# A fused pooled-attention and two-expert kernel: one of three Strassen sums moved from GpSimd to VectorE, attention steps split in two, loads handed out later

## The chip, the core and the metric

The kernel runs on one core of a Trainium2 chip. The time is device microseconds (us) of one execution; the number to predict is the median of the changed kernel's runs. TensorE is called PE (its weight loads PEld), VectorE DVE, ScalarE ACT, GpSimd POOL, SyncE SP. SP issues nearly all DMAs. Each engine works through its own queue in the order in which the program was written.

## The reference

```
k_p, v_p = k and v averaged over groups of 8 positions      # 8 batches, 8 heads, 576 x 64 -> 72 x 64
attn = softmax(q @ k_p.T / 8) @ v_p                          # per batch and head
x = attn as 4608 tokens x 512
h = x @ w_in                      # 512 x 2048
x = (h * clip(h + 3, 0, 6) / 6) @ w_out
out = (silu(x @ w_gate) * (x @ w_val)) @ w_out2              # d_ff 1536
```

All inputs arrive as 64-bit floats in raw words; the kernel itself turns weights into 32-bit floats ("rescale", then "join").

## The kernel before

Every matrix product is done in split form: an operand is a high part, rounded to the matmul's format, and a low part (the rest), and three matmuls make one product. Every operand is therefore written twice: ACT copies the high part, DVE (or POOL) subtracts to get the low part.

The program has four stages, one after the other on PE.

1. **Startup**: attention of the first 512 tokens.
2. **The up stage**: the first layer's up product for nine blocks of 512 tokens, 16 pieces f of 128 hidden units each (`up`, L587, twelve 512-column matmuls). While block j is multiplied, the attention of block j+1 is woven in. After each piece ACT forms relu (`act1`, L598, tile `t`) and DVE the gated value (L600, tile `g`), which is stored to DRAM.
3. **The down stage**: the first layer's down product (L850), 63 steps i = 7j + n, in Strassen form with seven products per block. The sums S1 to S4 of quarters of g are needed. In the kernel before, S3 = g11 - g21 is formed by POOL in the up stage, in the tile before it is stored (L602, for the 8 pieces f < 8 of each block); S2, S1 and S4 are formed by DVE in the down stage (`sum_b`, L828).
4. **The second expert** (L671 and what is around it), which the diff doesn't touch.

The attention of a unit (a head pair p of a batch b, 64 to 256 tokens) is cut into steps with letters: S scores, X subtract the maximum, A exponential, N row sums, M scale on POOL (L522), E the split of the last 16 columns, T transposes on PE, U and L the split of the transposed weights, V the value product on PE (L565 to L568, bank `psv`), W the high part of its result on ACT (L576), Y the low part on DVE (L580, tile `x`). There is a single `psv` bank, so the value product of a unit waits for the Y of the unit before. Once per head pair there are K steps (RK sums the keys on POOL, L382; K transposes them) and value steps: R0 sums the values on POOL (tile `v_in`, L425, L432), R1 their tail (tile `vts`, L425), R splits both (ACT L144 and L441, DVE L145 and L442, tiles `vst` and `vtl`), and then the loads for the second head pair after it are issued. A table `when` gives each letter a place (units later, place within the unit), and the steps are sorted by it; `attn_slot` deals them out, two slots per piece f, by their PE steps S, V, T. The weights of later stages are prepared besides (`prep_step`): loads, rescale on ACT, join on DVE (L136, L139), sums on POOL (L202, L207), a high-part copy of 1792 elements on ACT (L261), a low part on DVE (L264), a store.

The lines around the gate in the main loop:

```
up(hp, wu[f], x_tile(j))
attn_slot(j, 2 * f)
g = act1(f, hp)
attn_slot(j, 2 * f + 1)
```

Of the kernel before, what the change touches and what calls it, by code (L numbers as in the profile page):

```python
# [8 lines left out]
F32 = mybir.dt.float32  # L9
# [14 lines left out]
def kernel(  # L24
# [28 lines left out]
    P = 128  # L53
# [20 lines left out]
    t_p = l1.enter_context(tc.tile_pool(name="t", bufs=3))  # L74
# [13 lines left out]
    def big_w(name):  # L88
        return wu_p.tile([P, BIG], F32R, tag="w4", name=name)

# [56 lines left out]
    class Weights:  # L147
# [14 lines left out]
        def convert(self):  # L162
# [63 lines left out]
    def prep_step(u, step):  # L226
# [21 lines left out]
        elif step == 2:  # L248
            q = prep_t["f", u] = q7_p.tile([P, 8, WH], F32, tag="q7", name="q7")
            for s, at in prep_t.pop(("q", u)):  # L250
                join(s, q[:, at].bitcast(I32), 2)
        elif step == 3:
# [5 lines left out]
        elif step == 4:  # L258
            q, t = prep_t["f", u], s7_p.tile([P, 7, 2, WH], F32R, tag="s7", name="s7")
            prep_t["s", u] = t  # L260
            nc.scalar.copy(out=t[:, :, 0], in_=q[:, :7])  # L261
        else:
            q, t = prep_t.pop(("f", u)), prep_t.pop(("s", u))
            nc.vector.tensor_tensor(out=t[:, :, 1], in0=q[:, :7], in1=f32(t[:, :, 0]), op=ALU.subtract)  # L264
# [107 lines left out]
    def reduce_k(b, p):  # L372
        kp = a_p.tile([SP_, 2, D], F32, tag="kp", name="kp", bufs=1)
# [63 lines left out]
    def split_v(b, p):  # L437
        w, m = vst_t[p], vm_t.pop((b, p))
        split(w[:, 0], w[:, 1], m, nc.vector)
        w, vt = vtl_t[p][:, D:], vt_t.pop((b, p))  # L440
        nc.scalar.activation(out=w, in_=vt[:, 0], func=ACTF.Copy, scale=1.0 / POOL)  # L441
# [82 lines left out]
    def split_tail(u, engine):  # L524
        e, _, et, _ = e_t[u]
        qt, ni = e.shape[0], e.shape[1]
        tail = e[:, :, P:K2]
        r = et.rearrange("q i (r s) -> q i r s", r=3)[:, :, :, :TAIL]
        nc.scalar.copy(
            out=r[:, :, 0::2].bitcast(F32R), in_=tail.unsqueeze(2).to_broadcast([qt, ni, 2, TAIL])  # L530
        )
        engine.tensor_tensor(out=r[:, :, 1], in0=tail, in1=r[:, :, 0], op=ALU.subtract)
# [288 lines left out]
    SLOT = {"11": 0, "S1": 0, "12": 1, "S4": 1, "S3": 2, "22": 3, "S2": 3}  # L821
# [8 lines left out]
    def split_b(i, c):  # L830

        j, n = divmod(i, 7)
        if j < NB:
            t = gb[i, c] = gb_p.tile([P, 2, CB, MB], F32R, tag="gb", name="gb")
# [62 lines left out]
    for j in range(NB):  # L897
# [38 lines left out]
    }  # L936
    events = []
    for i in range(NU):
# [4 lines left out]
        stages = [(what, i) for what in "SXANMETULVWY"]  # L943
# [4 lines left out]
        if i in first_in_head:  # L948
            stages += [(what, first_in_head[i]) for what in ("RK", "K", "R0", "R1", "R")]
# [17 lines left out]
    for i, u in enumerate(units):  # L967
        h, sg = head_no[u[:2]], seg_no[seg_of[u]]
        before(*((what, i) for what in "SXANMETULVWY"))
        before(("P", sg), ("S", i))  # L970
        before(("RK", h), ("K", h), ("S", i))
        before(("R0", h), ("R", h), ("V", i))
# [7 lines left out]
        if h + 1 < len(heads):  # L980
            before(("K", h), ("RK", h + 1))
# [279 lines left out]
```

## Time and profile before

| what | us |
|---|---|
| runs of the kernel before | 1894.56, 1894.41, 1892.64 (median 1894.41) |
| the profiled execution, its own time | 1893.08 |
| its span, first to last instruction | 1891.3 |
| up stage, from 50 to 721 | 671.0, of it PE busy 567.05 |
| down stage, from 721 to 1084 | 363.0, of it PE busy 362.77 |
| second expert, from 1084 to 1891 | 807.0, of it PE busy 793.21 |

An engine's busy time beside the length of a stage tells how far that engine is from filling it. The granted clock is the mean over a stretch; TensorE runs at one of two levels, 1.2 and 2.4 GHz, and 1.00 means the higher one all the time.

### The profile page before, as it was taken

What the parts mean: (1) busy time and instruction counts of PE and PEld (TensorE: products, weight loads), DVE (VectorE), ACT (ScalarE), POOL (GpSimd) and SP (SyncE); (2) the same over time, 40 slices, a digit from 0 to 9 for tenths busy, and PEclk for the clock granted to TensorE, in tenths of its full rate; (3) what the DMA queues carried; (4) which work ended last, traced back from release to release, by engine and by line L of the source; (5) the groups of instructions that cost most, each with busy time, mean ns of one, the idle gap of its engine ahead of it and who ended that gap; (6) DMA issues with size and microseconds to landing.
All of it is one profiled execution on the core that took longest, in us unless ns stands there. A gap on an engine that the chain in (4) does not pass through costs nothing.

```text
span 1891.3 us, 31360 instructions
## 1 busy us (share of the span) xinstructions
PE 1750.4 (93%) x11241; PEld 1641.4 (87%) x11241; DVE 1334.1 (71%) x2398; ACT 758.3 (40%) x1689; POOL 695.3 (37%) x899
## 2 busy tenths in 40 slices
PE   5877878878797989999999989999999999999999
PEld 4666757767676879999999989999999999999999
DVE  6665757778776726778878666866867767668666
ACT  6553434444453524554555422422423324224223
POOL 5445366576765310000000036155054153351460
PEclk7889989989898999999999989999999999999999
DMA  7744667766765788654555377787887887977876
GB/s 167 170 128 140 199 186 208 246 192 218 227 200 168 257 299 324 224 182 173 179 181 195 108 279 255 260 315 237 292 287 247 292 291 239 318 264 249 291 245 218
DMA packets 235836, 432.52 MB, mean 229 GB/s; under 512 B 86688, under 2 KB 168608, under 8 KB 218528
## 3 DMA queue, kind: packets, MB, share of 16 engines
q1 hardware_dynamic: 229184, 425.00, 68.4%
q10 hardware_dynamic: 6496, 5.51, 0.9%
q8 instruction: 89, 1.46, 0.3%
q14 instruction: 67, 0.55, 0.1%
HBM read 326.11 MB, written 104.33 MB: 228 GB/s over the span
## 4 chain that ended last, share of the span: by engine, by line
PE 71%; DMA 8%; DVE 8%; POOL 4%; ACT 3%; SPq 3%; issue 3%; POOLq 0%; DVEq 0%; ACTq 0%
PE b L671 42%; PE b L850 17%; PE h L587 10%; DMA g<-g 3%; DMA q_in<-in_q_dram 2%; DVE g L600 2%; ACT t L598 1%; POOL vts L425 1%; SPq L366 1%; DMA wstg<-in_moe_w_out_dram 1%; POOL v_in L425 1%; POOL g L602 1%; POOL q L207 1%; SPq L118 1%; DMA wstg<-in_moe_w_gate_dram 1%
## 5 line engine op out<-in xcount | busy, mean ns | idle before, releaser
L671 PE MATMUL b<-xc,wr 128*128 128x384 f32 x3024 | 529.4, 336 | 10.2 <-DMA wr<-sup 6.5
L671 PEld LDWEIGHTS b<-xc,wr 128*128 128x128 f32 x3024 | 527.2, 189 | 11.3 <-ACT xc L144 9.4
L587 PE MATMUL h<-x,wu 128*128 128x512 f32 x1728 | 458.8, 420 | 6.9 <-DVE g L600 6.9
L718 POOL TENSOR_TENSOR s<-s,c 128x384 f32<-128x384 f32 x144 | 142.4, 1012 | 770.1 <-ACT s L716 770.1
L587 PEld LDWEIGHTS h<-x,wu 128*128 128x128 f32 x1728 | 340.7, 203 | 79.4 <-DVE g L600 8.3
L680 DVE TENSOR_TENSOR c<-c,b 128x384 f32<-128x384 f32 x504 | 265.2, 552 | 178.9 <-PE b L671 153.6
L850 PEld LDWEIGHTS b<-gb,pw 128*128 128x128 f32 x3024 | 362.3, 191 | 0.6 <-DVE gb L145 0.3
L850 PE MATMUL b<-gb,pw 128*128 128x256 f32 x3024 | 362.7, 283 | 0.1
L671 PE MATMUL b<-wr,gc 128*128 128x256 f32 x2268 | 265.6, 279 | 0.0
L671 PEld LDWEIGHTS b<-wr,gc 128*128 128x128 f32 x2268 | 265.4, 188 | 0.0
L144 ACT CAST gb<-gq 128x512 fp32r<-128x512 f32 x252 | 155.4, 621 | 175.8 <-PE b L850 154.4
L145 DVE TENSOR_TENSOR gb<-gq,gb 128x512 fp32r<-128x512 f32 x252 | 168.5, 689 | 74.4 <-ACT gb L144 73.1
L600 DVE SCALAR_TENSOR_TENSOR g<-t,h 128x512 f32<-128x512 f32 x144 | 98.0, 682 | 141.9 <-ACT t L598 98.7
L725 POOL TENSOR_TENSOR gf<-s,c 128x384 f32<-128x384 f32 x144 | 168.2, 1192 | 67.2 <-DVE c L680 64.5
L144 ACT CAST gc<-gf 128x768 fp32r<-128x768 f32 x126 | 105.6, 838 | 186.9 <-POOL gf L725 100.9
L716 ACT ACTIVATE s<-c 128x384 f32<-128x384 f32 x144 | 73.5, 526 | 204.5 <-DVE c L680 203.3
L145 DVE TENSOR_TENSOR gc<-gf,gc 128x768 fp32r<-128x768 f32 x126 | 133.8, 1095 | 15.6 <-ACT gc L144 13.9
L598 ACT ACTIVATE t<-h,half 128x512 f32<-128x512 f32 x144 | 98.5, 684 | 114.3 <-PE h L587 99.5
L565 PE MATMUL psv<-aT,vst 128*128 128x256 f32 (+3 forms) x96 | 32.6, 339 | 90.3 <-DVE x L580 80.5
L565 PEld LDWEIGHTS psv<-aT,vst 128*128 128x128 f32 x96 | 19.6, 204 | 101.3 <-DVE x L580 31.6
L602 POOL TENSOR_TENSOR g<-g 128x256 f32<-128x256 f32 x72 | 57.1, 795 | 121.5 <-DVE g L600 112.3
L522 POOL TENSOR_TENSOR e<-e,sm 96x288 f32<-96x288 f32 (+3 forms) x85 | 58.8, 692 | 106.6 <-DVE sm L518 69.9
(106 smaller groups left out, 1824.5 us busy)
## 6 DMA issues: line engine op xcount, KB each, us to landing
wr<-sup SPq DMA_DIRECT2D x72, 1024.0 KB
wr<-sdn SPq DMA_DIRECT2D x84, 768.0 KB
wr<-sup SPq DMA_DIRECT2D x72, 768.0 KB
gq<-g SPq DMA_DIRECT2D x36, 1024.0 KB
g<-g SPq DMA_DIRECT2D x128, 256.0 KB
sup<-s SPq DMA_DIRECT2D x12, 1792.0 KB
wstg<-in_moe_w_out_dram SPq DMA_DIRECT2D x56, 256.0 KB
sw<-s SPq DMA_DIRECT2D x8, 1792.0 KB
```

What stands on the lines that cost most here:

```text
L144: nc.scalar.copy(out=hi, in_=src)
L145: lo_engine.tensor_tensor(out=lo, in0=src, in1=f32(hi), op=ALU.subtract)
L587: nc.tensor.matmul(out=ps, lhsT=w(kt, wh), rhs=x(kt, xh), start=first and n == 0, stop=last and n == 3 * len(kts) - 1,)
L598: nc.scalar.activation(out=t, in_=ps, func=ACTF.Relu, bias=half, scale=1.0 / 6.0)
L600: nc.vector.scalar_tensor_tensor(out=g, in0=t, scalar=1.0, in1=ps, op0=ALU.min, op1=ALU.mult)
L602: nc.gpsimd.tensor_tensor(out=g[:, MB:], in0=g[:, :MB], in1=g[:, MB:], op=ALU.subtract)
L671: nc.tensor.matmul(out=ps, lhsT=w(wh), rhs=x(xh), start=first and n == 0, stop=last and n == 2)
L680: add = lambda dst, a, b: nc.vector.tensor_tensor(out=dst, in0=a, in1=b, op=ALU.add)
L716: nc.scalar.activation(out=g[q], in_=c[q], func=ACTF.Sigmoid)
L718: nc.gpsimd.tensor_tensor(out=g[q], in0=g[q], in1=c[q], op=ALU.mult)
L725: nc.gpsimd.tensor_tensor(out=gf[p][:, GP[TURN[q]], f], in0=g[q], in1=c[q], op=ALU.mult)
L850: nc.tensor.matmul(out=ps[:, d], lhsT=w[:, CB * c + k, wh, P * d:P * (d + 1)], rhs=g[:, gh, k], start=what == place and (c, d, k, m) == (0 ...
```

## The change

It is made of these parts.

- S3 is no longer formed by POOL before the store. `store_g` now stores the plain g21, and `sum_b` forms S3 on DVE in the down stage, in two halves at n = 0 of every block.
- The gate (`gate1`) is written after the second attention slot of a piece, its relu (`act1`) before it as it was. The ring of `g32` goes from 3 to 4 tiles and that of `t` from 3 to 2. The joined first-layer weights take their place in the ring `gb` and no longer in the ring of `t`.
- Value steps: R keeps the two ACT copies, a new step Q holds the two DVE low parts. Tail steps: E keeps the ACT copy, a new step F the low part. RK, M, R0, R1, R and W get other places in `when`; the ring of `kp` goes from 1 to 2.
- Weight preparation: six steps become nine; the join goes over two slots, the high-part copy and the low part are cut into 4 and 3 of their 7 planes.
- Key, tail and value loads go into the list `later`, eight steps behind RK or Q, and are issued from there. In the last block the load of the fourth weight operand is moved behind the loop, and the load of g21 forward.

```diff
-    t_p = l1.enter_context(tc.tile_pool(name="t", bufs=3))
+    t_p = l1.enter_context(tc.tile_pool(name="t", bufs=2))
...
-                t = t_p.tile([P, WC], F32, tag="t", name="w32")
+                t = f32(new_gb().rearrange("p a k n -> p (a k n)")[:, :WC])
...
-        for step, off in enumerate((0, 3, 4, 5, 6, 7)):
+        for step, off in enumerate((0, 3, 4, 5, 6, 7, 8, 8, 9)):
...
-            nc.scalar.copy(out=t[:, :, 0], in_=q[:, :7])
+            q, t, part = prep_t["f", u], prep_t["s", u], slice(0, 4) if step == 5 else slice(4, 7)
+            nc.scalar.copy(out=t[:, part, 0], in_=q[:, part])
...
-        kp = a_p.tile([SP_, 2, D], F32, tag="kp", name="kp", bufs=1)
+        kp = a_p.tile([SP_, 2, D], F32, tag="kp", name="kp", bufs=2)
...
     def split_v(b, p):
+        nc.scalar.copy(out=vst_t[p][:, 0], in_=vm_t[b, p])
+        nc.scalar.activation(
+            out=vtl_t[p][:, D:], in_=vt_t[b, p][:, 0], func=ACTF.Copy, scale=1.0 / POOL
+        )
+
+    def split_v_lo(b, p):
         w, m = vst_t[p], vm_t.pop((b, p))
-        split(w[:, 0], w[:, 1], m, nc.vector)
+        nc.vector.tensor_tensor(out=w[:, 1], in0=m, in1=f32(w[:, 0]), op=ALU.subtract)
...
-    def act1(f, ps):
+    def act1(ps):
         t = t_p.tile([P, N], F32, tag="t", name="t")
         nc.scalar.activation(out=t, in_=ps, func=ACTF.Relu, bias=half, scale=1.0 / 6.0)
-        g = t_p.tile([P, N], F32, tag="g32", name="g32")
+        return t
+
+    def gate1(t, ps):
+        g = t_p.tile([P, N], F32, tag="g32", name="g32", bufs=4)
         nc.vector.scalar_tensor_tensor(out=g, in0=t, scalar=1.0, in1=ps, op0=ALU.min, op1=ALU.mult)
-        if f < NP1:
-            nc.gpsimd.tensor_tensor(out=g[:, MB:], in0=g[:, :MB], in1=g[:, MB:], op=ALU.subtract)
         return g
...
-            "S2": ("22", "S3", ALU.subtract), "S1": ("S2", "11", ALU.add), "S4": ("12", "S2", ALU.subtract),
+            "S3": ("11", "21", ALU.subtract), "S2": ("22", "S3", ALU.subtract), "S1": ("S2", "11", ALU.add), "S4": ("12", "S2", ALU.subtract),
...
-        "RK": (-2, 14), "K": (-1, 11), "P": (-1, 4), "S": (1, 0), "X": (1, 1), "A": (1, 15), "N": (1, 18),
-        "M": (1, 19), "E": (2, 15), "T": (3, 16), "U": (4, 2), "L": (4, 15), "V": (5, 14),
-        "W": (5, 14.5), "Y": (5, 20.5), "R0": (1, 21), "R1": (2, 15), "R": (2, 19),
+        "RK": (-2, 3), "K": (-1, 11), "P": (-1, 4), "S": (1, 0), "X": (1, 1), "A": (1, 15), "N": (1, 18),
+        "M": (2, 2), "E": (2, 15), "F": (2, 18), "T": (3, 16), "U": (4, 2), "L": (4, 15), "V": (5, 14),
+        "W": (5, 16.5), "Y": (5, 20.5), "R0": (0, 21), "R1": (1, 15), "R": (2, 3), "Q": (2, 15),
...
+            later.append((done[0] + 8, lambda h=h: load_k(*heads[h], nc.sync)))
+
+    def next_v(i):
+        for load in (load_vtail, load_v):
+            for h in next_heads(i):
+                later.append((done[0] + 8, lambda load=load, h=h: load(*heads[h], nc.sync)))
...
-            ("g", 0, 0), ("w", 0, 0), ("w", 0, 1), ("g", 0, 3), ("w", 1, 0), ("w", 1, 1), ("w", 2, 0),
-            ("w", 2, 1), ("g", 0, 1), ("w", 3, 0), ("w", 3, 1), ("g", 0, 2)]))
+            ("g", 0, 0), ("w", 0, 0), ("w", 0, 1), ("g", 0, 3), ("w", 1, 0), ("w", 1, 1), ("g", 0, 2),
+            ("g", 0, 1), ("w", 2, 0), ("w", 2, 1)]))
...
-                g = act1(f, hp)
+                t = act1(hp)
                 attn_slot(j, 2 * f + 1)
+                g = gate1(t, hp)
...
-        for n in (4, 5, 6):
+        for n in (3, 4, 5, 6):
...
-        sums_at = {1: (("S2", 0), ("S2", 1)), 2: ((), ("S1", 0)), 3: (("S1", 1), ()),
+        sums_at = {0: (("S3", 0), ("S3", 1)), 1: (("S2", 0), ("S2", 1)), 2: ((), ("S1", 0)), 3: (("S1", 1), ()),
```

The order of PE's own instructions is the same in both kernels. What moves is the order on DVE, ACT, POOL and SP. The first place is on DVE, in the attention of batch 6, ahead of the low part of a value result (`x`), for which PE's next value product waits. Before, from the subtraction of the maximum (`e`) to that low part:

```order
L494 TENSOR_TENSOR e_5592<-pss_5588,mx_5590 128x144
L458 STREAM_TRANSPOSE qT_5598<-q_in_5475 128x448
L559 TENSOR_TENSOR aT_5594<-pst_5554,aT_5594 128x192
L532 TENSOR_TENSOR et1_135<-e_5504,et1_135 128x16
L516 TENSOR_REDUCE sm_5612<-e_5592 128x2
L517 TENSOR_SCALAR sm_5612<-sm_5612 128x2
L518 RECIPROCAL sm_5612<-sm_5612 128x2
L145 TENSOR_TENSOR vst1_124<-v_in_4897,vst1_124 128x128
L442 SCALAR_TENSOR_TENSOR vtl1_128<-vts1_132,vtl1_128 32x64
L580 TENSOR_TENSOR x_5155<-psv_5600,x_5155 128x192
L600 SCALAR_TENSOR_TENSOR g32_5667<-t_5665,h_5625 128x512
```

With the change, the same head pair's value steps and the low part of the unit that follows them:

```order
L506 TENSOR_TENSOR e_5570<-pss_5566,mx_5568 128x144
L470 STREAM_TRANSPOSE qT_5579<-q_in_5455 128x448
L452 TENSOR_TENSOR vst1_124<-v_in_4873,vst1_124 128x128
L454 SCALAR_TENSOR_TENSOR vtl1_128<-vts1_132,vtl1_128 32x64
L576 TENSOR_TENSOR aT_5572<-pst_5538,aT_5572 128x192
L620 SCALAR_TENSOR_TENSOR g32_5595<-t_5564,h_5525 128x512
L139 TENSOR_SCALAR q7_5522<-wstg_5280 128x512
L142 SCALAR_TENSOR_TENSOR q7_5522<-wstg_5280,q7_5522 128x512
L549 TENSOR_TENSOR et1_135<-e_5488,et1_135 128x16
L528 TENSOR_REDUCE sm_5593<-e_5570 128x2
L529 TENSOR_SCALAR sm_5593<-sm_5593 128x2
L530 RECIPROCAL sm_5593<-sm_5593 128x2
```

The next row on DVE is the low part of `x`. The value low parts (`vst`, `vtl`) stood right ahead of it before; now eight rows stand between, among them a gate and half a join.

The second place is on POOL, for the second and the third head pair of the same batch (values `v_in`, tails `vts`; the scaling M writes `e`). Before:

```order
L425 TENSOR_TENSOR v_in_4897<-v_in_4897 128x64
L432 TENSOR_TENSOR v_in_4897<-v_in_4897,vmask_133 128x128
L602 TENSOR_TENSOR g32_5585<-g32_5585 128x256
L425 TENSOR_TENSOR vts1_132<-vts1_132 96x256
L425 TENSOR_TENSOR vts1_132<-vts1_132 96x128
L425 TENSOR_TENSOR vts1_132<-vts1_132 96x64
L202 TENSOR_TENSOR q7_5536<-q7_5536 128x256 x4
L522 TENSOR_TENSOR e_5592<-e_5592,sm_5612 128x144
L425 TENSOR_TENSOR v_in_5569<-v_in_5569 128x256
```

With the change:

```order
L439 TENSOR_TENSOR v_in_4873<-v_in_4873,vmask_133 128x128
L534 TENSOR_TENSOR e_5411<-e_5411,sm_5438 128x144
L432 TENSOR_TENSOR vts1_132<-vts1_132 96x256
L432 TENSOR_TENSOR vts1_132<-vts1_132 96x128
L432 TENSOR_TENSOR vts1_132<-vts1_132 96x64
L549 TENSOR_TENSOR et0_134<-e_5411,et0_134 128x16
L432 TENSOR_TENSOR v_in_5548<-v_in_5548 128x256
L432 TENSOR_TENSOR v_in_5548<-v_in_5548 128x128
L432 TENSOR_TENSOR v_in_5548<-v_in_5548 128x64
L439 TENSOR_TENSOR v_in_5548<-v_in_5548,vmask_133 128x128
L534 TENSOR_TENSOR e_5488<-e_5488,sm_5517 128x144
```

The subtraction on `g32` and the block of preparation sums have left this stretch, and the values of the third head pair (`v_in_5548`) stand ahead of the scaling of `e_5488`. Its unit's scaling wrote `e_5504` before, and that one and the next unit's (`e_5592`) came ahead of the third pair's values (`v_in_5569`).

## Rows read from the trace of the kernel before

**Rows 1.** Windows: length, busy PE, PEld, DVE, ACT, POOL (instructions), granted clock, DMA share, GB/s

```profile
50.00:721.00 671.00, 567.05 (x2806) 466.51 (x2807) 449.00 (x1023) 296.16 (x841) 356.43 (x550) 0.92 0.66 206
721.00:1084.00 363.00, 362.77 (x3025) 362.15 (x3024) 284.59 (x406) 185.43 (x299) 0.00 (x0) 1.00 0.53 187
```

**Rows 2.** Waits of PE, 50 to 721: total us, times, longest

```profile
PE psv L565 <- DVE x L580: 80.5, 37, 7.4
PE psk L406 <- POOL kp L382: 8.7, 6, 2.4
PE h L587 <- DVE g L600: 6.9, 3, 4.1
```

**Rows 3.** Waits of ACT and of DVE, 50 to 721

```profile
ACT vtl L441 <- POOL vts L425: 40.6, 20, 6.5
ACT s L261 <- POOL q L207: 21.8, 7, 5.2
...
DVE g L600 <- DMA g<-g: 37.3, 9, 8.6
```

**Rows 4.** Timeline, 490 to 499, DVE, ACT, POOL and PE (start, us, instruction, idle before)

```profile
494.24 2.22 POOL L425 TENSOR_TENSOR vts<-vts 96x256 f32<-96x256 f32 x3
...
496.50 0.26 ACT L441 ACTIVATE vtl<-vts 96x64 fp32r<-96x64 f32 x1 [6.49 <-POOL vts L425]
...
498.33 0.36 DVE L580 TENSOR_TENSOR x<-psv,x 128x192 fp32r<-128x192 f32 x1
...
498.75 0.53 PE L565 MATMUL psv<-aT,vst 128*128 128x192 f32 x1 [7.43 <-DVE x L580]
```

**Rows 5.** Timeline of PE: first and last value product of two kinds of gap

```profile
77.40 0.39 PE L565 MATMUL psv<-aT,vst 128*128 128x64 f32 x1 [4.23 <-DVE x L580]
...
598.74 0.27 PE L565 MATMUL psv<-aT,vst 128*128 128x64 f32 x1 [2.23 <-DVE x L580]
...
66.84 0.27 PE L565 MATMUL psv<-aT,vst 128*128 128x64 f32 x1 [0.43 <-DVE x L580]
...
592.21 0.27 PE L565 MATMUL psv<-aT,vst 128*128 128x64 f32 x1 [0.75 <-DVE x L580]
```

**Rows 6.** Timeline of PE: first and last slow piece, between them one quick piece

```profile
50.91 4.54 PE L587 MATMUL h<-x,wu 128*128 128x512 f32 x12
...
487.77 2.94 PE L587 MATMUL h<-x,wu 128*128 128x512 f32 x12
...
599.18 4.33 PE L587 MATMUL h<-x,wu 128*128 128x512 f32 x12
```

**Rows 7.** Groups by line, 50 to 721, then 721 to 1084: busy, mean ns, idle before

```profile
L602 POOL TENSOR_TENSOR g<-g 128x256 f32<-128x256 f32 x72 | 57.1, 795 | 121.5 <-DVE g L600 112.3 <-DVE sm L517 5.9 <-DMA sup<-s 2.0
L828 DVE TENSOR_TENSOR gq<-gq 128x1024 f32<-128x1024 f32 x54 | 65.8, 1219 | 0.0
L145 DVE TENSOR_TENSOR gb<-gq,gb 128x512 fp32r<-128x512 f32 x251 | 167.8, 689 | 74.4 <-ACT gb L144 73.1
```

**Rows 8.** Joins and low parts by line, 50 to 721, then 721 to 1084

```profile
L136 DVE TENSOR_SCALAR q<-wstg 128x512 int32<-128x512 int32 x40 | 24.4, 610 | 0.0
L264 DVE TENSOR_TENSOR s<-q,s 128x1792 fp32r<-128x1792 f32 x20 | 40.5, 2027 | 0.0
...
L264 DVE TENSOR_TENSOR s<-q,s 128x1792 fp32r<-128x1792 f32 x6 | 12.1, 2020 | 0.0
L136 DVE TENSOR_SCALAR q<-wstg 128x512 int32<-128x512 int32 x12 | 5.1, 422 | 0.0
```

**Rows 9.** Timeline, a value load of SP and the POOL sum that waits for it

```profile
329.52 2.94 SPq L318 DMA_DIRECT2D vts<-in_v_dram  x3
...
339.03 1.24 POOL L425 TENSOR_TENSOR v_in<-v_in 128x256 f32<-128x256 f32 x1 [2.41 <-DMA v_in<-in_v_dram]
```

**Rows 10.** The same for the next head pair, POOL not waiting

```profile
340.48 1.49 SPq L318 DMA_DIRECT2D vts<-in_v_dram  x3
...
345.94 1.67 POOL L425 TENSOR_TENSOR v_in<-v_in 128x256 f32<-128x256 f32 x3
```

More of the change, by code (lines that the diff above doesn't have):

```diff
@@ L89, in big_w, with new_gb @@
         return wu_p.tile([P, BIG], F32R, tag="w4", name=name)
+    def new_gb():
+        return gb_p.tile([P, 2, 2, 256], F32R, tag="gb", name="gb")
     def big_x(name):
@@ L247, in prep_step @@
                 rescale(s)
[L248 to L252, printed above, removed]
+        elif step in (2, 3):
+            if step == 2:
+                prep_t["f", u] = q7_p.tile([P, 8, WH], F32, tag="q7", name="q7")
+            s, at = prep_t["q", u].pop(0)
+            join(s, prep_t["f", u][:, at].bitcast(I32), 2)
+        elif step == 4:
             q, eng = prep_t["f", u], nc.gpsimd if u < PREP_A else nc.vector
@@ L257, in prep_step @@
                 sums_b(eng, lambda n: q[:, B7[n]])
-        elif step == 4:
-            q, t = prep_t["f", u], s7_p.tile([P, 7, 2, WH], F32R, tag="s7", name="s7")
-            prep_t["s", u] = t
-            nc.scalar.copy(out=t[:, :, 0], in_=q[:, :7])
-        else:
-            q, t = prep_t.pop(("f", u)), prep_t.pop(("s", u))
-            nc.vector.tensor_tensor(out=t[:, :, 1], in0=q[:, :7], in1=f32(t[:, :, 0]), op=ALU.subtract)
+        elif step in (5, 6):
+            if step == 5:
+                prep_t["s", u] = s7_p.tile([P, 7, 2, WH], F32R, tag="s7", name="s7")
+            q, t, part = prep_t["f", u], prep_t["s", u], slice(0, 4) if step == 5 else slice(4, 7)
+            nc.scalar.copy(out=t[:, part, 0], in_=q[:, part])
+        else:
+            q, t, part = prep_t["f", u], prep_t["s", u], slice(0, 4) if step == 7 else slice(4, 7)
+            nc.vector.tensor_tensor(out=t[:, part, 1], in0=q[:, part], in1=f32(t[:, part, 0]), op=ALU.subtract)
+            if step == 7:
+                return
             if kind == "up":
@@ L522, in scale_e, with tail_of, split_tail @@
         nc.gpsimd.tensor_tensor(out=e3, in0=e3, in1=sm.to_broadcast(list(e3.shape)), op=ALU.mult)
-    def split_tail(u, engine):
+    def tail_of(u):
         e, _, et, _ = e_t[u]
-        qt, ni = e.shape[0], e.shape[1]
-        tail = e[:, :, P:K2]
-        r = et.rearrange("q i (r s) -> q i r s", r=3)[:, :, :, :TAIL]
+        return e[:, :, P:K2], et.rearrange("q i (r s) -> q i r s", r=3)[:, :, :, :TAIL]
+    def split_tail(u):
+        tail, r = tail_of(u)
+        qt, ni = tail.shape[0], tail.shape[1]
         nc.scalar.copy(
@@ L531, in split_tail, with lo_tail @@
         )
+    def lo_tail(u, engine):
+        tail, r = tail_of(u)
         engine.tensor_tensor(out=r[:, :, 1], in0=tail, in1=r[:, :, 0], op=ALU.subtract)
@@ L833, in split_b @@
         if j < NB:
-            t = gb[i, c] = gb_p.tile([P, 2, CB, MB], F32R, tag="gb", name="gb")
+            t = gb[i, c] = new_gb()
             split(t[:, 0], t[:, 1], gq[j, SLOT[DN[n][1]]][:, CB * c:CB * (c + 1)], nc.vector)
@@ L942 @@
             lag["A"] = (1, 1)
-        stages = [(what, i) for what in "SXANMETULVWY"]
+        stages = [(what, i) for what in "SXANMEFTULVWY"]
         if 2 <= i < 8:
@@ L948 @@
         if i in first_in_head:
-            stages += [(what, first_in_head[i]) for what in ("RK", "K", "R0", "R1", "R")]
+            stages += [(what, first_in_head[i]) for what in ("RK", "K", "R0", "R1", "R", "Q")]
         events += [(i + lag[st[0]][0], lag[st[0]][1], st[1], n, st) for n, st in enumerate(stages)]
@@ L968 @@
         h, sg = head_no[u[:2]], seg_no[seg_of[u]]
-        before(*((what, i) for what in "SXANMETULVWY"))
+        before(*((what, i) for what in "SXANMEFTULVWY"))
         before(("P", sg), ("S", i))
         before(("RK", h), ("K", h), ("S", i))
-        before(("R0", h), ("R", h), ("V", i))
+        before(("R0", h), ("R", h), ("Q", h), ("V", i))
         before(("R1", h), ("R", h))
@@ L1027, in do_step @@
             split_v(*heads[i])
-            for h in ((KT, KT + 1) if i == KT - 1 else (i + 2,)):
-                if KT <= h < len(heads) and i >= KT - 1:
-                    load_vtail(*heads[h], nc.sync)
-            for h in ((KT, KT + 1) if i == KT - 1 else (i + 2,)):
-                if KT <= h < len(heads) and i >= KT - 1:
-                    load_v(*heads[h], nc.sync)
+        elif what == "Q":
+            split_v_lo(*heads[i])
+            next_v(i)
         elif what == "P":
@@ L1059, in do_step @@
         elif what == "E":
-            split_tail(units[i], nc.vector if i % 2 else nc.gpsimd)
+            split_tail(units[i])
+        elif what == "F":
+            lo_tail(units[i], nc.vector if i % 2 else nc.gpsimd)
         elif what == "T":
@@ L1069, in run_steps @@
         while done[0] < upto:
-            while later and later[0][0] <= done[0]:
-                later.pop(0)[1]()
+            for due in [x for x in later if x[0] <= done[0]]:
+                later.remove(due)
+                due[1]()
             do_step(steps[done[0]])
```

15 lines of the change are left out of this document (7 added, 8 removed), and 2 rows, old and new, of the table when_startup.

## The prediction

> **What bounds the kernel now.** I read the stages first [rows 1]. In the down stage PE is busy 362.77 of 363.0 us at clock 1.00: nothing is to be had there. In the up stage it is busy 567.05 of 671.0 us at a mean clock of 0.92. So the up stage is where time can be won, and it has two kinds of it: idle time, 104 us, and slow time. No other engine fills the stage: DVE is at 449.00 us (67%), POOL at 356.43 (53%), ACT at 296.16 (44%). An idle PE among engines that are all half idle is a matter of order and waiting.
>
> The waits of PE name the place [rows 2]: 80.5 us in 37 waits are value products held by DVE's low part of the unit before (there is one `psv` bank), 8.7 us are key transposes held by POOL's key sum, 6.9 us are up products held by the gate. DVE is not slow at that low part; it comes to it late. The waits of ACT and DVE say why [rows 3]: ACT stood 40.6 us for POOL's sum of the value tails and 21.8 us for POOL's preparation sums; DVE stood 37.3 us for a store to free a gate tile. The largest gap shows the chain [rows 4]: POOL runs its tail sums from 494.24, ACT stands 6.49 us at `vtl` until 496.50, DVE's value split waits behind, and `x` comes at 498.33 with PE idle for 7.43 us.
>
> I sorted the gaps over 0.25 us by what stood still in the 3 us ahead of them. 18 value-product gaps, first and last in [rows 5], have ACT standing at a value copy or a preparation copy for POOL: 57.7 us. 18 others, the next two rows there, have no such wait: 27.7 us. They come from plain queue order on DVE.
>
> The clock is the second loss. A piece of twelve matmuls takes 2.94 us at the higher of the two levels; 18 of the 131 pieces that I could see whole took over 3.4 us, first and last in [rows 6], together 82.9 us against 18 x 2.99 us for the mean of the quick ones: 29 us. All but the first stand behind a gap.
>
> **Part by part, against the profiled 1893.08 us.**
>
> *Value steps apart, and earlier (R0, R1, R, Q).* R1 and R were one or two slots apart; now two to three, and R's low parts stand eight rows ahead of the `x` they used to delay. The 18 gaps of 57.7 us are the stake. ACT's wait was 40.6/20 = 2.0 us on average, about what the new distance gives, so most go; the copies that wait for preparation sums keep their distance of one piece and only gain from a lighter POOL. Bounds: nothing (each gap turns into another wait) and 57.7. A gap that is removed will often leave one of the small kind, 27.7/18 = 1.5 us. If about 12 leave one, 18 us remain: I take **-40**.
>
> *Key steps earlier, two `kp` tiles.* At stake 8.7 us [rows 2]; bounds 0 and 8.7. I take **-7**.
>
> *Gate in four tiles, not behind POOL's subtraction.* It ends up to 37.3 us of DVE's waiting for stores [rows 3]. On PE this shows as 6.9 us in the last block [rows 2], where up products follow each other with no attention between. There two loads are also moved out of the way. Bounds 0 and 6.9; **-5**. The ring of `t` shrinks to two: ACT then waits if DVE is two pieces late. The cover is two pieces, 5.9 us; without it each delay passes on whole.
>
> *W behind A and E, the gate behind the second slot, half joins.* These act on the 27.7 us. Some of the order gets better (a join no longer comes as one block), some worse (half a join now stands ahead of `x`). Bounds -20 and +9, a third lost or two thirds won; **-9**.
>
> *POOL loses the 72 subtractions,* 57.1 us [rows 7]. POOL is off the path but for the waits above, so no term of its own. DVE may gain as well: a join's shift took 610 ns beside a working POOL and 422 ns in the down stage where POOL does nothing [rows 8]. That is 40 x 0.19 = 7.5 us over the stage, of which a sixth goes with POOL's work (57.1 of 356.43): 1.2 us on an engine that is not full. The Trainium skill (SBUF — State Buffer, "Who interferes with whom") says that a VectorE instruction with two SBUF inputs and a GpSimd instruction that reads SBUF exclude each other outright. By that rule up to 57.1 x 449/671 = 38 us of DVE time would come free, an estimate by the page; the shift above shows 1.2, and the sum goes by the rows.
>
> *S3 on DVE in the down stage.* 18 new instructions of 128x1024 elements, the size of L828: 18 x 1.219 = 21.9 us [rows 7]. The cover is the 74.4 us that DVE stands there for ACT's copies. In a step of 363/63 = 5.76 us the four low parts take 2.76 us and two sums 2.44: 5.2. A preparation step of 2 us on top overdraws one step by some 1.5 us, and the four-tile ring is three chunks, 4.3 us, ahead. **0**; without cover +21.9. The load of g21 is now needed at n = 0 and issued at the end of n = 4 of the block before: two steps, 11.5 us.
>
> *Cut copies, joins and low parts.* The cost of one more instruction, from 512 elements in 689 ns and 1024 in 1219 [rows 7], is 689 - 530 = 159 ns. Two cuts for each of 20 preparations in the stage are 40 x 0.159 = 6.4 us, taken the same for ACT as for DVE, on engines at 44% and 67%: 0, bound +6.4. The Trainium skill speaks against the cut here (VectorE: DVE Perf Modes, "SBUF-src ops pay a fixed extra latency per instruction"): every small instruction pays a fixed cost again. The row agrees that there is one.
>
> *Loads eight steps later.* This is the cost. Head pairs that take one unit each come from batch 4 on. For eight of them (the third and fourth pair of batches 4 to 7) I counted the steps: the value load is handed out two steps before POOL's R0, in the same slot, where four slots lay between. POOL must then stand for the whole transfer. From SP's first tail load to POOL's first sum it was 9.5 us in the one case in which POOL waited [rows 9], and at most 5.5 us in the next [rows 10]. Behind R0 stands M, behind M the ACT copy of E; T and V come more than a unit later, about 6 us (a block of 671/9 = 75 us holds 12 units there), so PE feels only the rest, 0 to 4 us. I take 1.5 each: **+12**, bounds 0 and +38.
>
> *Clock.* With two thirds of the long gaps gone, 12 of 18 slow pieces go: 12 x 1.6 = **-19**. Bounds -29 and 0.
>
> Sum: -40 - 7 - 5 - 9 + 12 - 19 = -68; 1893.08 - 68 = 1825. The median of the runs lies 1.3 us above the profiled time, so **1826 us**. The startup and the second expert stay.
>
> **The rivals.**
>
> *The waits change owner* (same direction, less). DVE at 449 us has only 567 us of PE work to hide behind once PE's gaps close, and is then 75 to 80% full with an order that alternates with ACT. If half of the 57.7 us turns up as other waits on `x`, the order changes give nothing and the clock follows by half: -29 - 7 - 5 + 12 - 9 = -38, 1856 us. For it: the 18 gaps without any ACT wait, 1.5 us each, exist already. Against it: of the six gaps over 4.5 us five belong to the 18 with POOL in them.
>
> *POOL stands for the value loads and PE with it* (slower). If the slack of a unit is not there, each of the eight stalls of 9.5 us falls on PE and brings a slow piece: 8 x (9.5 + 1.6) = 89 us against 80 of gains (40 + 7 + 5 + 9 + 19): 1893 + 9, 1903 us. It turns the sign from 80/8 - 1.6 = 8.4 us per head pair on. For it: [rows 9]. Against it: [rows 10], and ACT's place for R two slots and more behind.
>
> *The change doesn't do it.* POOL is the late engine for another reason than its load, R1 is late by as much as it was moved, and gains and stalls balance: within 0.2% (3.8 us) of 1894. Against it: S3's removal alone takes 16% of POOL's work.
>
> *DVE fails in the down stage.* +21.9 on top of the forecast, 1848: still faster.
>
> *DVE comes free by more than the joins show.* If every subtraction of POOL held up DVE for its length while DVE had work, 38 us, and half of that lay on the path, another 19 us go: 1807. For it: the join's 610 beside 422 ns [rows 8]. Against it: a low part of 1792 elements takes the same in both stages (2027 and 2020 ns) [rows 8]. The rule of the SBUF page above is this one.
>
> **How the numbers follow.** Forecast with its bounds 0.60 (1790 to 1848; in it 0.05 for DVE failing in the down stage and 0.05 for DVE coming free by more), waits change owner 0.25 (1848 to 1886), no change 0.04, slower 0.08, all gaps and all slow pieces gone (below 1790) 0.03. Anything over 0.2%, about what a measurement of this kernel can tell from no change, counts as faster or slower: faster 0.88, same 0.04, slower 0.08. The range 1785 to 1878 leaves out slower, no change, the upper end of the second case and the lowest end.
>
> **What would show it.** Right: ACT's wait at `vtl` for POOL from 40.6 to under 10 us; PE's wait at `psv` from 80.5 to 35 to 45; DVE's wait for stores under 10; the up stage near 603 us at a clock of 0.95; the down stage still 363 with DVE near 306. New: POOL waiting at `v_in` for DMA eight times. Wrong: if PE's wait at `psv` stays over 65, the gain is under 30; if these eight waits show on PE one for one, it is gone; if the down stage is longer than 370, the cover for S3 was not there.

## The result, and the profile of the changed kernel

The changed kernel takes 1839.82 us (median of 4 runs, 1838.77 to 1842.25) beside 1893.53 us for the kernel before; the ratio is 0.9721, with a 95% interval of 0.9704 to 0.9738. It is faster by 53.7 us. Forecast were 1826 us and a gain of 68, with a range of 1785 to 1878.

The first view is that of the windows of the changed kernel, its up stage and its down stage (columns as in [rows 1]).

```profile
49.20:668.20 619.00, 550.55 (x2807) 457.38 (x2806) 438.89 (x1045) 297.39 (x858) 292.20 (x477) 0.94 0.72 221
668.20:1033.00 364.80, 362.70 (x3022) 361.85 (x3021) 301.12 (x426) 184.78 (x304) 0.00 (x0) 1.00 0.55 194
```

The up stage is 52 us shorter (619.0 for 671.0). PE is idle 68 us in it, not 104, and busy 16.5 us less at a clock of 0.94 for 0.92. POOL is 64 us less busy. The down stage is some 2 us longer, with DVE 16.5 us busier: S3 is paid there and nearly hidden. Not all of the gain lies in the up stage: the second expert takes 804.5 us to its end, for 807.3, and the startup ends 0.8 us earlier.

The second view is that of the waits in the up stage of the changed kernel, of PE, ACT, DVE and POOL in turn (total us, times, longest).

```profile
PE psv L582 <- DVE x L597: 56.7, 22, 5.8
PE psk L413 <- POOL kp L389: 4.0, 3, 1.7
PE h L604 <- DVE g L620: 3.6, 2, 2.9
...
ACT et L543 <- POOL e L534: 93.8, 33, 11.5
ACT vtl L446 <- POOL vts L432: 8.0, 7, 2.8
ACT x L593 <- PE psv L585: 6.4, 3, 2.3
...
DVE g L620 <- ACT t L615: 40.7, 25, 6.4
DVE g L620 <- DMA g<-g: 19.9, 4, 6.6
...
POOL v_in L432 <- DMA v_in<-in_v_dram: 40.6, 7, 11.1
```

PE's wait at the value product falls from 80.5 to 56.7 us, that at the key transpose from 8.7 to 4.0, that at the up product from 6.9 to 3.6 [rows 2]. ACT's wait for POOL's tail sums is nearly gone, 8.0 for 40.6; DVE's for stores is nearly halved, 19.9 for 37.3 [rows 3]. Two waits are new. POOL stands 40.6 us, in 7 waits, for value loads, which had been one wait of 2.4 us (that ACT's old wait had the same 40.6 us is chance). And ACT, which had waited 5.3 us in all for POOL at the tail copy `et`, now waits 93.8 us there.

The longest of these is told by the timeline of the changed kernel from 290 to 310.5 (start, length, instruction, idle before).

```profile
295.69 3.10 SPq L325 DMA_DIRECT2D vts<-in_v_dram  x3
...
298.83 1.30 SPq L318 DMA_DIRECT2D v_in<-in_v_dram  x1
...
304.96 1.65 POOL L432 TENSOR_TENSOR v_in<-v_in 128x256 f32<-128x256 f32 x3 [11.12 <-DMA v_in<-in_v_dram]
...
307.10 0.67 POOL L534 TENSOR_TENSOR e<-e,sm 128x288 f32<-128x288 f32 x1
...
307.79 0.24 ACT L543 CAST et<-e 128x64 fp32r<-128x64 f32 x1 [11.53 <-POOL e L534]
...
308.41 0.45 DVE L528 TENSOR_REDUCE sm<-e 128x4 f32<-128x288 f32 x1 [8.78 <-ACT e L521]
...
309.73 0.58 PE L582 MATMUL psv<-aT,vst 128*128 128x256 f32 x1 [4.68 <-DVE x L597]
```

It is read from the top. SP hands out the tail and value loads of a head pair from 295.69 on. POOL's program has the value sum next, and POOL stands 11.12 us until the values have landed. The scaling `e` behind it runs at 307.10; ACT, whose next instruction is the copy of that scaled tail, has stood 11.53 us; DVE stands 8.78 us for the exponentials behind ACT's copy; the low part of `x` comes late; PE has been idle for 4.68 us. Each of the four engines is held by the one instruction at the head of its queue.

I sorted the gaps of PE over 0.25 us as in the prediction. Those with ACT standing at a value copy or a preparation copy for POOL went from 18 and 57.7 us to 6 and 18.7 us; the other value-product and transpose gaps went from 18 and 27.7 us to 18 and 40.8 us. Of the whole pieces of twelve matmuls 13 of 113 are over 3.4 us, 20 us more than as many quick ones (18 of 131 and 29 us before). Counted over all 144 pieces of either trace it is 15 pieces and 25 us, before 20 and 34: the same 9 us.

### The profile page after: what moved, and what is told of

It is laid out like the page before. It is cut to its first block, busy times and chain, and to the rows that moved or that the text cites. A ratio compares the mean times of both kernels' runs of the same rounds, so it can differ in the third digit from the quotient of the medians.

```text
span 1837.5 us, 31222 instructions
## 1 busy us (share of the span) xinstructions
PE 1733.2 (94%) x11241; PEld 1631.4 (89%) x11241; DVE 1342.0 (73%) x2442; ACT 759.7 (41%) x1715; POOL 632.0 (34%) x827
## 4 chain that ended last, share of the span: by engine, by line
PE 77%; DMA 8%; DVE 7%; POOL 2%; ACT 2%; SPq 2%; issue 1%; DVEq 0%; ACTq 0%; POOLq 0%
PE b L689 43%; PE b L868 19%; PE h L604 12%; DMA g<-g 2%; DMA q_in<-in_q_dram 1%; DVE g L620 1%; DMA y<-o 1%; PE pss L483 1%; DMA sw<-s 1%; DMA v_in<-in_v_dram 1%; POOL v_in L432 1%; SPq L373 1%; DVE s L269 1%; DVE mx L489 0%; ACT t L615 0%
## 5 line engine op out<-in xcount | busy, mean ns | idle before, releaser
L604 PE MATMUL h<-x,wu 128*128 128x512 f32 x1728 | 448.5, 412 | 4.8 <-DVE g L620 3.6
L604 PEld LDWEIGHTS h<-x,wu 128*128 128x128 f32 x1728 | 333.3, 199 | 75.4 <-DVE g L620 5.0
L148 DVE TENSOR_TENSOR gc<-gf,gc 128x768 fp32r<-128x768 f32 x126 | 133.8, 1094 | 15.6 <-ACT gc L147 13.9
L534 POOL TENSOR_TENSOR e<-e,sm 96x288 f32<-96x288 f32 (+3 forms) x85 | 53.5, 629 | 141.7 <-DVE sm L530 77.2
L706 ACT COPY c<-b 128x384 f32<-128x384 f32 x72 | 34.0, 472 | 144.0 <-PE b L689 140.2
L582 PE MATMUL psv<-aT,vst 128*128 128x256 f32 (+3 forms) x96 | 33.0, 344 | 59.1 <-DVE x L597 56.7
L846 DVE TENSOR_TENSOR gq<-gq 128x1024 f32<-128x1024 f32 x72 | 87.8, 1219 | 0.0
```

The lines of the kernel that those rows point to most:

```text
L148: lo_engine.tensor_tensor(out=lo, in0=src, in1=f32(hi), op=ALU.subtract)
L604: nc.tensor.matmul(out=ps, lhsT=w(kt, wh), rhs=x(kt, xh), start=first and n == 0, stop=last and n == 3 * len(kts) - 1,)
L846: nc.vector.tensor_tensor(out=v(what), in0=v(a), in1=v(b), op=op)
```

## The experiments

All times are medians of four runs beside the kernel before on the same chip (1892.5 to 1894.9 us; three chips were used). The four runs of one kernel lie 2 to 8 us apart, so a difference of 3 us or less between two experiments is not shown to be one. "Loads at once" is the second experiment's kernel, from which most of the others take away one part.

**S3 alone.** The kernel before, with S3, the one of the four sums S1 to S4 that POOL formed, moved to the down stage and nothing else.

```diff
-        if f < NP1:
-            nc.gpsimd.tensor_tensor(out=g[:, MB:], in0=g[:, :MB], in1=g[:, MB:], op=ALU.subtract)
...
+            "S3": ("11", "21", ALU.subtract),
...
-        sums_at = {1: (("S2", 0), ("S2", 1)),
+        sums_at = {0: (("S3", 0), ("S3", 1)), 1: (("S2", 0), ("S2", 1)),
```

> The kernel before with S3 alone moved to VectorE in the down stage. Theory (POOL's subtraction was on the path only through the stores and a little through POOL's lateness): 1880 to 1890, down stage still 363 us. Rival 1 (POOL's lateness was the root of all): half of the 54 us or more, 1866 or less. Rival 2 (S3 on VectorE costs in the down stage): 1895 to 1915.

1867.05 us, ratio 0.9867 (0.985 to 0.9883): 26.5 us of the 53.7, about twice the most that the theory gave. The first row is the up stage among the windows of that kernel, the second its wait of ACT for the tail sums.

```profile
50.10:691.40 641.30, 556.96 (x2805) 461.77 (x2804) 432.16 (x1021) 294.28 (x837) 296.23 (x477) 0.93 0.69 214
```

```profile
ACT vtl L441 <- POOL vts L425: 12.5, 14, 2.3
```

Two things are to be seen. ACT's wait for the tail sums falls from 40.6 to 12.5 us although sum and copy stand where they stood. And DVE does nearly the same instructions of the stage (1021 for 1023) in 432.16 us, not 449.00: 16.8 us less, with nothing else changed in the stage than the 72 subtractions that left POOL.

More has left POOL with them than 57.1 us of work. A subtraction needs the gate of its piece, and POOL stood 112.3 us for gates in front of these 72 [rows 7], with all that was written behind them; in the order of POOL before, one stands right ahead of the tail sums. So it was in the largest gap [rows 4], where this row comes just before the tail sums.

```profile
493.56 0.72 POOL L602 TENSOR_TENSOR g<-g 128x256 f32<-128x256 f32 x1 [3.88 <-DVE g L600]
```

Of the 40.6 us that ACT stood for the tail sums, POOL stood 6.3 in front of a subtraction, ran subtractions for 7.0 and the tail sums for 23.9, as I count in the trace. Four things thus go together in this run: less work on POOL, no standing for the gate, a faster DVE, and stores that need not wait for POOL (DVE's wait for stores falls from 37.3 to 26.8 us). No run takes them apart; the one that is missing leaves the subtraction on POOL at a place where its gate is long done.

**Loads at once.** The changed kernel, tail and value loads handed out right behind Q and not eight steps later.

```diff
-                later.append((done[0] + 8, lambda load=load, h=h: load(*heads[h], nc.sync)))
+                load(*heads[h], nc.sync)
```

> The changed kernel with the tail and value loads issued at once behind the value split, not eight steps later. Theory (POOL's 40.6 us of standing for value loads, in 7 waits of up to 11.1 us, reaches PE through the scaling and ACT's tail copy and costs some 17 us of PE gaps): the waits shrink by about the eight steps, 3 to 4 us each, and 5 to 10 us come back: 1830 to 1835. Rival (the waits are hidden, and loads ahead of a store hold up SP): within 3 us of 1840, or above it.

1820.56 us, ratio 0.9617 (0.9603 to 0.9631): 19.3 us faster than the changed kernel, twice the most that was expected. The rows are the waits of POOL and ACT of that kernel that were new.

```profile
POOL v_in L432 <- DMA v_in<-in_v_dram: 20.9, 6, 5.4
```

```profile
ACT et L543 <- POOL e L534: 72.6, 34, 7.5
```

POOL's wait for value loads halves, and the longest falls from 11.1 to 5.4 us. So the late loads were a loss. The rest of ACT's wait, 72.6 us, does not come from the late loads: it falls to 1.6 us in the run below that puts the scaling M (with F and W) back in its earlier place.

**Loads at once, value sums later.** The kernel of the last experiment, with R0 half a unit later.

```diff
-        "R0": (0, 21), "R1"
+        "R0": (1, 8), "R1"
```

> As the run with the loads at once, and POOL's value sum R0 half a unit later, so that 16 steps lie between load and sum and no longer 2. Theory: POOL's wait for value loads falls from 40.6 to under 10 us, PE's wait at the value product from 56.7 to about 40, 1822 to 1830. Rival (value sum and tail sum now stand close together on POOL, and ACT waits for POOL at the value copies again as in the kernel before): ACT's wait there rises from 8 to over 25 us and the time stays at 1836 or above.

1814.44 us, ratio 0.9584 (0.9566 to 0.9602). POOL's wait for loads is 13.8 us and PE's wait at the value product 35.2, both in the direction of the theory, and the time is better than it had it; ACT's wait at `et` falls to 24.3. The rival's wait comes too, in part: ACT stands 18.1 us at the tail sums, not 6.3.

**Value steps back.** Loads at once, and R0, R1, R and Q where they were.

```diff
-"R0": (0, 21), "R1": (1, 15), "R": (2, 3), "Q": (2, 15),
+"R0": (1, 21), "R1": (2, 15), "R": (2, 19), "Q": (2, 19),
```

> The changed kernel with the value steps back in their old places (sum, tail sum, split and low part one right behind the other, low part in front of the low part of x) and the loads at once. Theory (the value steps were the largest term, 58 us of gaps before, 19 left): ACT's wait at the tail copy comes back to 30 us or more, the gaps of that kind grow by 25 to 40 us, the waits for value loads go, net 1852 to 1868. Rival (what won was POOL's lighter load, the gate and the ring of four, and the value steps would have come right by themselves): 1830 to 1842.

1822.34 us, ratio 0.963 (0.9615 to 0.9644), 1.8 us more than with the value steps in their new places, which is within the spread. ACT's wait at the tail sums is 18.6 us, not 6.3, and far from the 40.6 of before. Sorted as above, the gaps of PE with ACT standing for POOL rise from 2 and 9.2 us to 8 and 22.8, while the other value-product and transpose gaps fall from 21 and 38.7 us to 17 and 29.1: the waits change owner. The theory falls: the step that I took for the largest term is worth next to nothing, here at least, where S3 has left POOL. The old places have a gain of their own, longer distances from load to sum, which may hide part of what they lose. What the value steps alone would do to the kernel before, no run shows.

**Gate back, preparation back, unit steps back, keys back.** Four kernels, each with loads at once and one part undone. The edits: the gate in front of the second slot; the six whole preparation steps of the kernel before; M, F and W in their old places; RK in its old place with one `kp` tile and its loads at once.

```diff
+                g = gate1(t, hp)
                 attn_slot(j, 2 * f + 1)
-                g = gate1(t, hp)
...
-        for step, off in enumerate((0, 3, 4, 5, 6, 7, 8, 8, 9)):
+        for step, off in enumerate((0, 3, 4, 5, 6, 7)):
...
-        "M": (2, 2), "E": (2, 15), "F": (2, 18),
+        "M": (1, 19), "E": (2, 15), "F": (2, 15),
-        "W": (5, 16.5),
+        "W": (5, 14.5),
...
-        "RK": (-2, 3),
+        "RK": (-2, 14),
```

> The kernel with the loads at once (1820.56), and the gate back in front of the second attention slot, the rings as in the changed kernel. Between S3 alone (1867.05) and this kernel 46 us are open, in four parts undone one by one here. Theory (the order of the unit's own steps holds most of the 46): the gate holds little, 1820 to 1829. Rival (the gate stood on VectorE in front of the low part of x and waited for ACT's relu, 98.7 us before, 38.4 now): 1832 to 1845.

1835.34 us, ratio 0.9687 (0.967 to 0.9705): the gate's place is worth 14.8 us, the rival's answer. The rows are the wait of DVE at the gate in the kernel before, and then the waits of DVE and of PE in this one.

```profile
DVE g L600 <- ACT t L598: 98.7, 69, 3.9
```

```profile
DVE g L620 <- ACT t L615: 101.5, 75, 5.9
```

```profile
PE psv L582 <- DVE x L597: 54.8, 30, 5.1
```

With the gate in front of the slot DVE stands 101.5 us for ACT's relu (38.4 with loads at once), and the attention's instructions of that slot stand behind it. PE waits 54.8 us for the low part of `x`, not 45.2.

> The kernel with the loads at once, and the weight preparation in six steps again, joins, copies and low parts whole. Theory (unit steps hold most): VectorE and ACT are held for at most 2.0 and 1.7 us at a time, less than a unit has in hand, 1820 to 1828. Rival (the whole pieces stood ahead of x on VectorE and were a cause of gaps): 1832 to 1845, PE's wait at the value product up by over 10 us. By the fixed price of an instruction, 159 ns, the whole pieces would win back at most 6 us: 1814.

1811.33 us, ratio 0.9557 (0.9534 to 0.9579). Whole preparation steps are 9.2 us faster than cut ones, more than the 6 us that the price of an instruction gives and well below the theory's 1820. The rows are the low parts of the preparation in the up stage, cut in the changed kernel and whole in this one.

```profile
L269 DVE TENSOR_TENSOR s<-q,s 128x1024 fp32r<-128x1024 f32 x20 | 25.7, 1284 | 0.0
L269 DVE TENSOR_TENSOR s<-q,s 128x768 fp32r<-128x768 f32 x20 | 22.0, 1099 | 0.0
```

```profile
L267 DVE TENSOR_TENSOR s<-q,s 128x1792 fp32r<-128x1792 f32 x20 | 40.7, 2037 | 0.0
```

A cut costs DVE 1284 + 1099 - 2037 = 346 ns here, and ACT 1046 + 834 - 1691 = 189 ns by the same rows of its copies. The 159 ns had been read in the down stage, where POOL does nothing; there a cut low part takes 1219 + 953 ns beside 2020 whole [rows 8], 152 more. The cut gives something back in the down stage, which takes 369.1 us with whole steps and 365.3 with cut ones (loads at once).

> The kernel with the loads at once, and the unit's steps M, F and W back in their old places (tail's low part right behind its copy, the high part of x right behind the value product). Theory (ACT stood 110.4 us for the value product before and 6.4 now, and what came behind it was late): 1835 to 1850, ACT's wait for the value product over 80 us. Rival (that wait was PE's own pace and cost nothing): 1818 to 1828.

1823.11 us, ratio 0.9626 (0.9606 to 0.9646): 2.6 us more, within the spread. The rows are two waits of ACT in that kernel.

```profile
ACT x L593 <- PE psv L585: 77.0, 50, 4.5
...
ACT et L543 <- POOL e L534: 1.6, 6, 0.4
```

ACT's wait at W comes back with 77.0 us (6.4 with loads at once), and the time is that of the rival. But M and F went back too, and the 72.6 us of ACT's wait for POOL at `et` are gone with them. So the two waits change places at the same time; that the one at W is PE's own pace and costs nothing by itself is not shown.

> The kernel with the loads at once, and the key steps back: key sum eleven places later, one tile for it, key loads at once. Theory (PE waited 8.7 us for key sums before, 3.3 now): 1822 to 1830. Rival (hidden): 1817 to 1822. Other rival (SP held up by key loads that wait for POOL, 34.9 us before, delays the query loads and the stores): 1832 to 1845.

1820.1 us, ratio 0.9609 (0.9592 to 0.9626): the same as with the key steps in their new places. PE's wait at the key transpose is 1.2 us, less than the 3.3 with loads at once: the key steps are hidden.

**S3 back.** Loads at once, with POOL's subtraction in the up stage again.

```diff
+        if f < NP1:
+            nc.gpsimd.tensor_tensor(out=g[:, MB:], in0=g[:, :MB], in1=g[:, MB:], op=ALU.subtract)
...
-        sums_at = {0: (("S3", 0), ("S3", 1)), 1: (
+        sums_at = {1: (
```

> The kernel with the loads at once (1820.56), and S3 formed by POOL in the up stage again, the store behind it. S3 alone gave 26.5 us on the kernel before. Theory (POOL's lateness is the root, and the new places of the steps lean on a POOL that is ahead): at least those 26 us are lost, 1845 to 1875, ACT's wait for POOL at the tail copies or at the scaling up by over 30 us. Rival (the new places have made the kernel proof against a late POOL): 1825 to 1840.

1855.78 us, ratio 0.9809 (0.9794 to 0.9823): 35.2 us lost. The rows are the waits of POOL, ACT and PE of that kernel.

```profile
POOL g L622 <- DVE g L620: 89.4, 32, 9.0
```

```profile
ACT et L543 <- POOL e L534: 117.9, 48, 9.3
```

```profile
PE psv L582 <- DVE x L597: 62.0, 27, 6.8
```

POOL stands 89.4 us for gates again, ACT waits 45 us more at `et` for a POOL that is late, and PE 17 us more for `x`. The tail sums are no longer where ACT waits (7.9 us): with the new places the lateness comes out at another copy.

**S3 and the gate alone.** The kernel before with S3 moved, the gate behind the second slot and its rings; the joined first-layer weights have to go into the ring `gb` with it.

```diff
-                g = act1(f, hp)
+                t = act1(hp)
                 attn_slot(j, 2 * f + 1)
+                g = gate1(t, hp)
...
+        g = t_p.tile([P, N], F32, tag="g32", name="g32", bufs=4)
```

> The kernel before with two parts of the change alone: S3 on VectorE, and the gate behind the second slot with its rings of four and two. Theory (these two hold most of the gain, 26.5 and 15 us undone singly): 1845 to 1855, PE's wait at the value product about 50 us. Rival (they need the other parts, since 36 us of the sum of single parts is missing): 1858 to 1868. Other rival (they alone make the whole of it, and all the other parts together give nothing): 1820 to 1835.

1838.87 us, ratio 0.9726 (0.9706 to 0.9746): as fast as the whole change. The gate with its rings adds 28.2 us to S3's 26.5. The up stage and the down stage of that kernel:

```profile
50.40:660.50 610.10, 542.34 (x2804) 452.48 (x2804) 431.12 (x1021) 293.39 (x837) 295.48 (x477) 0.95 0.72 222
660.50:1029.70 369.20, 365.31 (x3025) 363.90 (x3023) 303.53 (x424) 185.46 (x299) 0.00 (x0) 1.00 0.54 190
```

Its up stage is 9 us shorter than that of the changed kernel and has DVE 8 us less busy, with 24 instructions fewer. Its down stage is 4 us longer than that of the changed kernel, and 6 us longer than in the kernel before. DVE's wait for ACT's relu is 36.8 us.

**Rings back.** Loads at once, three tiles each for relu and gate.

```diff
-    t_p = l1.enter_context(tc.tile_pool(name="t", bufs=2))
+    t_p = l1.enter_context(tc.tile_pool(name="t", bufs=3))
...
-        g = t_p.tile([P, N], F32, tag="g32", name="g32", bufs=4)
+        g = t_p.tile([P, N], F32, tag="g32", name="g32")
```

> The kernel with the loads at once, and three tiles each for relu and gate again. Theory (VectorE's wait for stores, 23.0 us, sits in the last block and costs PE 3.5): 1820 to 1828, up by at most 6 us. Rival (a store that lands late holds up VectorE all through the stage): 1830 or more. Other rival (ACT wins by a third tile of relu): under 1818.

1827.1 us, ratio 0.9656 (0.9642 to 0.967): the rings are worth 6.5 us, at the edge of the theory.

**Both better parts together.** Loads at once, value sums later, preparation whole.

> A kernel meant to beat both: loads at once, value sums half a unit later, weight preparation in six whole steps. If the two gains found singly on the kernel with the loads at once (6 us for the later sums, 9 us for the whole preparation) add up: 1802 to 1808. If they fill the same gaps: 1809 to 1816.

1806.7 us, ratio 0.9552 (0.9533 to 0.9572): the fastest of all, 33.1 us below the changed kernel and 85.8 us below the kernel before on its chip. The two gains of 6.1 and 9.2 us together give 13.9, so they nearly add up.

## Why the prediction was right, and where its terms were not

The sign and the stage held, and the time lies in the stated range: 52 of the profiled 54 us came out of the up stage, out of its idle time and its slow pieces, and the down stage took S3 almost for nothing. The size was 14 us short. That the sum came so near is luck in part, for its terms erred both ways and the largest of them did not bring what it was put down for. Of the signs, ACT's wait at `vtl` (8.0 us), the waits for value loads (7 for 8) and the down stage came as written; PE's wait at `psv` (56.7, not 35 to 45), DVE's wait for stores (19.9, not under 10) and the up stage (619.0 us at 0.94, not 603 at 0.95) came part of the way. The rival of the waits that change owner, 1856 us, missed by 16 us and has its share: 39 us of the gaps that were named went, and 13 us of the others came.

*Value steps, -40.* The gaps it named went from 57.7 to 18.7 us, as much as it said, but not through this part. Sorted in the same way they are 42.3 us with S3 alone and 35.5 with S3 and the gate, and this part undone costs 1.8 us. The failed step is that gaps of PE were put down to ACT's wait for POOL because ACT stood at that time. In the largest gap the prediction has DVE's value split wait behind ACT; it did not. The rows are DVE in that gap.

```profile
492.59 0.31 DVE L458 STREAM_TRANSPOSE qT<-q_in 128x128 f32<-128x128 f32 x1 [4.85 <-DMA q_in<-in_q_dram]
...
493.67 0.90 DVE L136 TENSOR_SCALAR q<-wstg 128x512 int32<-128x512 int32 x1
...
496.32 0.69 DVE L139 SCALAR_TENSOR_TENSOR q<-wstg,q 128x512 int32<-128x512 int32 x1
...
497.55 0.27 DVE L145 TENSOR_TENSOR vst<-v_in,vst 128x128 fp32r<-128x128 f32 x1
497.85 0.45 DVE L442 SCALAR_TENSOR_TENSOR vtl<-vts,vtl 32x64 fp32r<-32x64 f32 x1
```

DVE stood 4.85 us for a query load and then had no pause until `x` at 498.33: a gate, a low part of the transposed weights, a whole join of four instructions, row sums, the value split. ACT's copy `vtl` was done at 496.76 [rows 4], before DVE came to its low part. Over the stage DVE stood 26.2 us for ACT's value copies, less than half of the 57.7 us that were set as the stake.

```profile
DVE vtl L442 <- ACT vtl L441: 14.1, 13, 3.8
...
DVE vst L145 <- ACT vst L144: 12.1, 4, 5.5
```

These are 5.5 and 5.7 us with S3 alone, 0.6 and 3.7 in the changed kernel.

*POOL loses the subtractions, no term of its own.* Measured are 26.5 us added alone and 35.2 us undone. I called POOL off the path but for its waits, and gave those waits to another part; S3 alone takes ACT's wait for the tail sums from 40.6 to 12.5 us with the distance left as it was. And I counted the 57.1 us of the subtractions, not the 112.3 us that POOL stood in front of them, in the same row. The sentence that DVE gains 1.2 us was wrong too: its work in the stage fell by 16.8 us with S3 alone, between this and the 38 us of the case that I gave 0.05.

*Gate in four tiles, -5, and its place within the -9.* Measured are 28.2 us for place and rings on top of S3, 14.8 for the place undone and 6.5 for the rings. The prediction never asked what stood behind the gate on DVE while it waited for ACT's relu: 98.7 us before, 36.8 with S3 and the gate moved, 101.5 with the gate back.

*Half joins, copies in two, within the -9 and 0.* They cost 9.2 us. The 6.4 us of fixed prices were named as a bound and called hidden by engines at 44% and 67%; the price itself was too low beside a working POOL (346 ns for a cut low part on DVE, not 159). The other value-product and transpose gaps fall from 38.7 to 32.6 us when the steps are whole again (loads at once).

*Late loads, +12.* Right by mechanism and too small: 19.3 us, 40.6 us of standing in 7 waits where 8 were forecast, the longest 11.1 us for the 9.5 assumed. The unit in hand covered less than I thought.

*Keys, -7.* The wait fell from 8.7 to 4.0 us, but not through this part: with the key steps back (loads at once) it is 1.2 us, and the time is the same.

*Clock, -19.* The excess of slow pieces went from 29 to 20 us, 9 of it won, in proportion to the gaps that stayed.

*S3 in the down stage, 0.* It is 1.8 us in the changed kernel and 2.6 with S3 alone, but 6 where the gate is moved and the preparation whole, in three kernels (369.1 to 370.0 us). The rows are two groups of DVE in the down stage of the changed kernel.

```profile
L148 DVE TENSOR_TENSOR gb<-gq,gb 128x512 fp32r<-128x512 f32 x249 | 165.6, 688 | 59.2 <-ACT gb L147 58.9
L846 DVE TENSOR_TENSOR gq<-gq 128x1024 f32<-128x1024 f32 x72 | 87.8, 1219 | 0.0
```

There are 18 more sums of 1219 ns, and DVE's idle time falls from 74.4 to 59.2 us [rows 7]: the cover was there.

*The second expert stays.* It is 2.8 us shorter, but not with S3 and the gate alone (807.1 us); which part does it, no run tells.

What stays open, beside what S3 is worth by which way, is the sum of the single parts. S3 and the gate make 53.6 us together beside the kernel before on their chip, the whole of the change. With the value loads at once the other parts give 18.3 us more, but undone one by one they come to 1.8, 2.6 and 0 us, and the cut preparation to a loss of 9.2. Some 23 us by these medians, of runs on three chips, come only from several of them together, or from the order of the last loads, which was not undone alone. No run tells which.

## What to carry to other kernels

When one engine waits for another, ask first whether the other is late because of its load or because of what stands ahead in its queue; the wait's row names the last instruction and says neither. An instruction weighs on its queue with its own time and with the time for which it stands at the head: 57.1 and 112.3 us for the subtractions. Two waits at the same time are not yet cause and effect: ask whether the engine between them stood still. Before a wait at the head of a queue is called harmless, list what stands behind it: 101.5 us at the gate were worth 15, while 71 us more at the value product and 71 us less at the tail copy made together no difference that these runs show. And a load handed out later must be followed to its first reader on every queue.

## What the hardware showed unasked

DVE's work shrank when POOL's did. The first row is the low part of the value tails in the up stage of the kernel before; the others are from the kernel with S3 alone, where the order on DVE is the same.

```profile
L442 DVE SCALAR_TENSOR_TENSOR vtl<-vts,vtl 32x64 fp32r<-32x64 f32 x28 | 23.5, 841 | 14.7 <-ACT vtl L441 14.1 <-ACT wstg L130 0.2
```

```profile
L264 DVE TENSOR_TENSOR s<-q,s 128x1792 fp32r<-128x1792 f32 x20 | 40.6, 2030 | 0.0
...
L136 DVE TENSOR_SCALAR q<-wstg 128x512 int32<-128x512 int32 x40 | 22.0, 549 | 0.0
...
L442 DVE SCALAR_TENSOR_TENSOR vtl<-vts,vtl 32x64 fp32r<-32x64 f32 x28 | 17.7, 633 | 6.5 <-ACT vtl L441 5.5 <-ACT wstg L130 0.2
```

The low part of the value tails, 64 elements long, takes 633 ns for 841, the shift of the join 549 for 610 [rows 8], and 422 in the down stage where POOL does nothing. In the changed kernel they are 469 and 477, but there the instructions also stand at other places, and the second half of the join takes 871 ns for 813. The Trainium skill (SBUF — State Buffer, "Who interferes with whom") says that a VectorE instruction with two SBUF inputs and a GpSimd instruction that reads SBUF contend for a shared port, which is an exclusive lock. The runs agree by direction: 57.1 us of work taken off POOL freed 16.8 us of DVE. But the whole low part of a preparation, two SBUF inputs as well, takes 2030 ns for 2027, and 2020 where POOL does nothing [rows 8]. That it is this port, and not another cause, no run here isolates.
